# Sixteen score pairs and twenty-four matmul slots: two ways to lay out the gaps of a filled group

## The chip, the cores and the metric

The kernel runs on one core of one Trainium2 chip. The metric is the device time of one execution in microseconds. Before the change it is 1833.53 us, the median of three runs (1833.28 to 1835.45).

## The reference, cut to what matters

One transformer block on a sequence of S = 2048 rows of D = 512 in float32: 32 heads of 16, full softmax attention, then a gated feed-forward layer of width F = 1792. Both halves are modulated by vectors computed from a condition `c`.

```python
h = _layernorm(x, axis=-1) * (1 + ca) + sa
x = x + ga * _A_ref(h, A_wqkv, A_wo)     # scores = q k^T * scale; p = softmax(scores); (p v) @ wo
h = _layernorm(x, axis=-1) * (1 + cb) + sb
x = x + gb * _B_ref(h, B_w_gate, B_w_up, B_w_down)   # (silu(h w_gate) * (h w_up)) @ w_down
```

## The kernel before

**Attention.** The sequence is cut into NC = 4 chunks of CW = 512 query columns, the heads into NG = 8 groups of four. A unit is one group of four heads for one chunk; there are 32 units, and a unit has 16 steps, one for each tile of 128 keys. A step has four heads. For each head there is a *score* (`score`, lines 566 to 575): a matmul of 50 rows into one PSUM bank (L573), from which ScalarE (ACT) makes the exponential into SBUF (L575). Because the softmax subtracts a maximum of each query, each score needs a *max* matmul some 21 steps ahead (`LEAD`), in `max_one` (lines 515 to 526): a matmul of 48 rows into a bank (L524), which VectorE (DVE) reduces over its 512 columns (L526). The probabilities times V are matmuls of 32 columns each (`pv_step`, L588), four heads side by side.

**Pairs.** `pair_of` (line 983) issues one score and one max together. The two use opposite halves of the array's rows (0 to 63 and 64 to 127), so that they run side by side. There are 16 x 4 pairs to a unit.

**Banks.** `Turn` hands out banks in rotation. In a filled stretch the scores alternate between two banks, 4 and 5, and the maxima rotate over three, 0, 1 and 2 (`four, bank = three, Turn(4, 5)`, line 1066). So score k may only start when the exponential of score k-2 has read its bank, and max k when the reduce of max k-3 has.

**Plain and filled stretches.** After attention of a chunk is done, its output projection and feed-forward layer are worked off inside the attention of the next chunk. `plain` (line 1047) issues pairs and probability-times-V steps alone. `filled` (line 1062) issues pairs, and behind pair r it takes `places[r]` *slots* of other work; after the last pair come the postponed element-wise steps (`hook`) and a burst of `len(places) // 2 + 2` half-steps of probability times V:

```python
        for r in range(len(places)):
            pair_of()
            take(work, places[r])
            if r % 4 == 3:
                end_steps()
        hook()
        pvs(len(places) // 2 + 2, False)
```

A slot is one step of the generator `accumulate` with `halves=True` (line 785 on): two matmuls of 64 rows (L790), one in each row half, again side by side. A job of `gate_up` or `out_pair` has 24 slots: twelve terms in each of two phases. In the first phase the upper row half accumulates into one output bank and the lower into the other; in the second they change over. Where `trade` is set, the change-over needs a wait: a no-op on ACT (L799) waits for the last matmuls of the first phase, and the first matmuls of the second phase wait for that no-op.

`filled_tile` (line 1078) lays out a job of `gate_up` or `out_pair`. Normally it takes one group of sixteen pairs with the tuple `FOUR`, and trades; near the end of a unit and near the end of the kernel it takes two groups of eight pairs with `TWO`. A `down` job has 12 slots in a group of eight pairs with `DOWN = (0, 3, 3, 0, 3, 3, 0, 0)`, and trades as well. In `FOUR` before, the first phase of twelve slots ends behind pair 6, then come pair 7 with no slot and pair 8, and then the second phase starts.

After a gate-up job ACT makes a tanh (L863) and DVE two products (L867, L869) from the two output banks. Once in a unit the maxima found ahead are gathered (in filled stretches by `max_turned`, line 546): a small reduce on DVE, a scale on ACT (L564), two small steps on DVE and eight small DMAs, each hung on a pair.

All engines run in program order, so the order in which these functions issue is the order of the work on TensorE.

Of the kernel before, what the change touches and what calls it, by code (L numbers as in the profile page):

```python
# [50 lines left out]
STARTS = (147, 275, 403)  # L51
TWO = (0, 3, 2, 2, 2, 2, 1, 0)
DOWN = (0, 3, 3, 0, 3, 3, 0, 0)
FOUR = (0, 3, 2, 2, 2, 1, 2, 0, 2, 2, 2, 2, 2, 1, 1, 0)
ALONE = {TWO: (0, 4, 0, 4, 0, 4, 0, 0), DOWN: (0, 6, 0, 0, 0, 6, 0, 0)}


# [47 lines left out]
def block_kernel(ctx, tc, x, wqkv, wo, w_gate, w_up, w_down, c, w_mod, out):  # L105
# [956 lines left out]
    def filled(places, work):  # L1062

        nonlocal four, bank, beside
        beside = True
        four, bank = three, Turn(4, 5)
        if done >= 4 * n - 4 * (LEAD - 1):
            places, bank = ALONE.get(places, places), Turn(4, 5, 0, 1, 2)
# [7 lines that stand above are left out]
        turns_behind()  # L1076

    def filled_tile(job, ch, arg):
        one = done // 4 % 16 != 15 and done + 16 <= 4 * n - 4 * (LEAD - 1)
        work = job(ch, arg, outs, True, one)  # L1080
        for places in (FOUR,) if one else (TWO, TWO):
            filled(places, work)
# [115 lines left out]
```

## Time and profile before

| | |
|---|---|
| median of the runs | 1833.53 us |
| profiled execution, its own time | 1833.51 us |
| its span, first to last instruction | 1831.6 us |
| TensorE (PE) busy | 1820.9 us, 99% |
| VectorE (DVE) busy | 1516.8 us, 83% |
| ScalarE (ACT) busy | 1246.8 us, 68% |
| GpSimd (POOL) busy | 460.8 us, 25% |
| granted TensorE clock | 1.000 |

The page gives the busy time of each engine, and the chain of waits that ended last, followed back from the last instruction. PE is a matmul, PEld the load of its weights; a weight load carries the wait of its matmul. A timeline gives start and duration of each instruction; neighbours of the same kind on one engine are merged (x4), and in brackets stands the idle time of the engine ahead of it and what ended that. Matmuls overlap, so a matmul's duration is longer than its distance from the next one, and a delay is seen in the starts. A matmul that comes right behind its own weight load has a longer duration than one whose weights were loaded ahead.

### The profile page before, as it was taken

To read this page: it belongs to the slowest core of one execution; us is meant where nothing else is said; L and a number is where in the kernel's file an instruction comes from. 1 tells how busy PE (TensorE), PEld (TensorE's weight loads), DVE (VectorE), ACT (ScalarE), POOL (GpSimd) and SP (SyncE) were. 2 spreads that over 40 slices of the span, in tenths; PEclk is the share of its full clock that TensorE was granted. 3 is DMA by queue.
4 is the path that set the end of the run, shared out by engine and by line. 5 is a ranking of instruction groups with operands and counts; after the bars stand their busy time and mean duration, and the time that the engine had idled before them with its cause. 6 is when DMAs were issued, how large, how long until landed. Compare 5 with 4: busy or idle time off the path is not lost.

```text
span 1831.6 us, 41022 instructions
## 1 busy us (share of the span) xinstructions
PE 1820.9 (99%) x16898; PEld 1196.8 (65%) x16898; DVE 1516.8 (83%) x2556; ACT 1246.8 (68%) x2357; POOL 460.8 (25%) x538
## 2 busy tenths in 40 slices
PE   9999999999999999999999999999999999999999
PEld 7876444444465777776565777776564677677887
DVE  6578999999999888888989888898989988922544
ACT  4223888888888666676888776676888867773211
POOL 3612544556223111111123111111213111030200
PEclk9999999999999999999999999999999999999999
DMA  9884876667745454453545554444643565233742
GB/s 313 280 226 146 205 200 166 179 170 209 191 85 120 103 125 140 126 133 73 156 95 131 115 125 118 123 115 90 161 79 57 125 146 122 105 118 121 279 168 104
DMA packets 80596, 267.63 MB, mean 146 GB/s; under 512 B 19744, under 2 KB 24320, under 8 KB 59728
## 3 DMA queue, kind: packets, MB, share of 16 engines
q1 hardware_dynamic: 61432, 179.71, 33.9%
q0 software_dynamic: 18288, 84.49, 19.2%
q8 instruction: 133, 2.18, 0.5%
q10 hardware_dynamic: 688, 0.80, 0.1%
q14 instruction: 55, 0.45, 0.1%
HBM read 201.85 MB, written 62.13 MB: 144 GB/s over the span
## 4 chain that ended last, share of the span: by engine, by line
PE 83%; DVE 14%; ACT 2%; DMA 0%; issue 0%; SPq 0%; DVEq 0%
PE bank L588 21%; PE bank L790 19%; PE bank L573 15%; DVE mx L526 14%; PE bank L524 11%; PE bank L809 8%; PE bank L214 7%; PE bank L852 1%; PE bank L773 0%; DMA wm_ab<-in_w_mod 0%; PE bank L166 0%; ACT sq L833 0%; DVE v_flat L883 0%; PE bank L538 0%; ACT sq L829 0%
## 5 line engine op out<-in xcount | busy, mean ns | idle before, releaser
L526 DVE TENSOR_REDUCE mx<-bank 128x1 f32<-128x512 f32 x2048 | 1269.3, 681 | 121.9 <-PE bank L524 83.5
L573 PE MATMUL bank<-qop,kop 50*128 50x512 f32 x2048 | 739.8, 428 | 1.4 <-ACT pu__17793 L575 0.2
L524 PE MATMUL bank<-kop,qop 48*128 48x512 f32 x2048 | 729.6, 425 | 0.3
L573 PEld LDWEIGHTS bank<-qop,kop 50*128 50x128 f32 x2048 | 345.7, 184 | 181.1 <-issue 37.4
L524 PEld LDWEIGHTS bank<-kop,qop 48*128 48x128 f32 x2048 | 345.3, 184 | 108.5 <-DVE mx L526 61.9
L790 PE MATMUL bank<-act,wgu 64*128 64x512 f32 x1872 | 306.0, 392 | 0.0
L790 PEld LDWEIGHTS bank<-act,wgu 64*128 64x128 f32 x1872 | 194.4, 187 | 24.1
L614 POOL TENSOR_TENSOR rb<-o,rb 128x512 f32<-128x512 f32 x31 | 39.9, 1286 | 539.1 <-DMA rb<-d_dr 400.0
L790 PE MATMUL bank<-wd,mid 64*128 64x512 f32 x912 | 131.6, 391 | 0.0
L871 POOL CAST mid<-m 128x512 fp32r<-128x512 f32 x40 | 24.4, 611 | 357.9 <-DVE m L869 357.9
L790 PEld LDWEIGHTS bank<-wd,mid 64*128 64x128 f32 x912 | 91.4, 186 | 11.7
L214 PE MATMUL bank<-hT,wqs 128*128 128x512 f32 x384 | 94.2, 397 | 0.4 <-DVE wqs L354 0.4
L867 DVE SCALAR_TENSOR_TENSOR q<-th,bank 128x512 f32<-128x512 f32 x56 | 38.1, 680 | 54.1 <-ACT th L863 54.1
L214 PEld LDWEIGHTS bank<-hT,wqs 128*128 128x128 f32 x384 | 70.6, 188 | 18.8 <-issue 3.1
L863 ACT ACTIVATE th<-bank 128x512 f32<-128x512 f32 x56 | 33.3, 594 | 57.9 <-PE bank L809 57.9
L883 DVE TENSOR_TENSOR x<-bank,x 128x512 f32<-128x512 f32 x84 | 53.9, 685 | 16.1 <-PE bank L790 16.1
L869 DVE TENSOR_TENSOR m<-bank,q 128x512 f32<-128x512 f32 x56 | 38.7, 692 | 21.7 <-PE bank L809 19.7
L872 POOL TENSOR_TENSOR mid<-m,mid 128x512 fp32r<-128x512 f32 x40 | 51.4, 1285 | 3.3
L809 PE MATMUL bank<-wd,mid 128*128 128x512 f32 x216 | 51.3, 393 | 0.0
L790 PE MATMUL bank<-wgu,act 64*128 64x512 f32 x288 | 48.2, 392 | 0.0
L214 PE MATMUL bank<-wqs,hT 128*128 128x512 f32 x192 | 48.0, 398 | 0.0
L809 PEld LDWEIGHTS bank<-wd,mid 128*128 128x128 f32 x216 | 40.4, 188 | 8.9
(6300 smaller groups left out, 5143.6 us busy)
## 6 DMA issues: line engine op xcount, KB each, us to landing
wgu<-gu_dr SPq DMA_DIRECT2D x48, 1024.0 KB
wd<-wd_dr SPq DMA_DIRECT2D x28, 1024.0 KB
kop<-kd SPq DMA_DIRECT2D x33, 768.0 KB
kop<-kd POOLq DMA_DIRECT2D x29, 768.0 KB, 8.7
gu_dr<-wgu POOLq DMA_DIRECT2D x14, 1024.0 KB, 12.7
kd<-prt SPq DMA_DIRECT2D x16, 512.0 KB
qd<-prt SPq DMA_DIRECT2D x16, 512.0 KB
kop<-gu_dr SPq DMA_DIRECT2D x8, 1024.0 KB
```

The lines of the kernel that those rows point to most:

```text
L214: nc.tensor.matmul(pt, lhs(a, k), rhs(b, k), start=(n == 0), stop=(n == 3 * nk - 1))
L524: nc.tensor.matmul(pm, qop[u][rows, s, qt * P:(qt + 1) * P], kop[u % 3][rows, s, kc * CW:(kc + 1) * CW], start=True, stop=True)
L526: nc.vector.tensor_reduce(mx[u][:, b, s, qt, kc:kc + 1], pm, op=ALU.max, axis=AX.X)
L573: nc.tensor.matmul(sp, kop[u % 3][rows, h // 2, kt * P:(kt + 1) * P], qop[u][rows, h // 2, :], start=True, stop=True)
L588: nc.tensor.matmul(pv[u][32 * h:32 * h + 32, cols], v_flat[:, e0:e0 + 32], p_[h][:, cols], start=(kt == 0 and half == 0), stop=(kt == 15), ...
L614: mul.tensor_mul(rb, o, rb)
L790: mm = nc.tensor.matmul(outs[e], lhs(e, a, k)[rows], rhs(b, k)[rows], start=(ph == 0 and j == 0), stop=(j == z and (ph == 1 or trade)), sk ...
L809: nc.tensor.matmul(outs[e], lhs(e, a, k), rhs(b, k), start=(j == 0), stop=(j == z))
L867: nc.vector.scalar_tensor_tensor(q, th, 1.0, outs[0], op0=ALU.add, op1=ALU.mult)
L869: nc.vector.tensor_mul(m32, outs[1], q)
L872: (nc.gpsimd if slow else nc.vector).tensor_sub(mid[:, 1, :], m32, mid[:, 0, :].bitcast(F32))
L883: nc.vector.tensor_add(ch.x2[:, t, :], outs[e], ch.x2[:, t, :])
```

## The change

The tuple `FOUR` says how many slots stand behind each of the sixteen pairs of a group. The sum (24) stays, and so does the number of slots ahead of pair 7 (12).

```diff
-FOUR = (0, 3, 2, 2, 2, 1, 2, 0, 2, 2, 2, 2, 2, 1, 1, 0)
+FOUR = (0, 3, 2, 1, 2, 1, 3, 0, 3, 1, 2, 1, 2, 1, 2, 0)
```

Taken two at a time, the neighbouring gaps before held 3 5 4 4 3 3 2 2 4 4 4 4 3 2 1 slots; now they hold 3 5 3 3 3 4 3 3 4 3 3 3 3 3 2. Behind the last pair of a group comes the burst of probability-times-V steps in both.

## The prediction

> **What bounds the kernel now.** I read the page first, then the views of lines L799 and L790 for the count of the groups, then the timeline of one group of sixteen pairs, and last a timeline of the neighbouring kinds of group for the price of the new spacing.
>
> ```profile
> span 1831.6 us, 41022 instructions
> PE 1820.9 (99%) x16898; PEld 1196.8 (65%) x16898; DVE 1516.8 (83%) x2556; ACT 1246.8 (68%) x2357; POOL 460.8 (25%) x538
> ...
> PE 83%; DVE 14%; ACT 2%; DMA 0%; issue 0%; SPq 0%; DVEq 0%
> ...
> L526 DVE TENSOR_REDUCE mx<-bank 128x1 f32<-128x512 f32 x2048 | 1269.3, 681 | 121.9 <-PE bank L524 83.5
> ```
>
> TensorE's order of instructions sets the end: 83% of the chain is PE. A "busy" PE at 99% hides small delays, because two row halves overlap; they have to be found in the starts. DVE is 14% of the chain, from the plain stretches, which this change leaves alone.
>
> How many groups does it touch? The trade of the banks leaves one ACT no-op (L799) in every group that trades: the FOUR groups and the down groups.
>
> ```profile
> L799 ACTq EVENT_SEMAPHORE x74: 17/17/17, 531.7 to 1662.7; - x74
> ```
> ```profile
> L790 PE MATMUL bank<-wd,mid x912: 384/392/471, 628.6 to 1664.1; 64*128 64x512 f32 x183
> ```
>
> A down job in halves is 12 slots of two matmuls: 912/24 = 38 jobs. So 74 - 38 = 36 FOUR groups use the edited tuple.
>
> Now one of them, from its first pair at 641.63 us. I number pairs from 0 and call gap k the slots behind pair k. First its start, then pairs 6 to 9 around the trade, then pairs 13 to 15 and the probability-times-V burst (L588) up to the next group.
>
> ```profile
> 641.63 0.50 PE L573 MATMUL bank<-qop,kop 50*128 50x512 f32 x1
> ...
> 641.97 0.39 PE L573 MATMUL bank<-qop,kop 50*128 50x512 f32 x1
> ...
> 642.20 1.89 DVE L526 TENSOR_REDUCE mx<-bank 128x1 f32<-128x512 f32 x3 [0.32 <-PE bank L524]
> ```
> ```profile
> 645.47 0.60 ACT L575 ACTIVATE pt__7527<-bank 128x512 f32<-128x512 f32 x1
> 645.48 0.42 PE L573 MATMUL bank<-qop,kop 50*128 50x512 f32 x1
> ...
> 645.74 0.64 PE L790 MATMUL bank<-act,wgu 64*128 64x512 f32 x4
> 645.96 0.60 ACT L575 ACTIVATE pt__7536<-bank 128x512 f32<-128x512 f32 x1
> ...
> 646.20 0.40 PE L524 MATMUL bank<-kop,qop 48*128 48x512 f32 x1
> ...
> 646.61 0.18 PEld L573 LDWEIGHTS bank<-qop,kop 50*128 50x128 f32 x1 [0.31 <-ACT pt__7536 L575]
> ...
> 646.62 0.50 PE L524 MATMUL bank<-kop,qop 48*128 48x512 f32 x1
> ...
> 646.95 0.64 PE L790 MATMUL bank<-act,wgu 64*128 64x512 f32 x4
> ...
> 647.31 0.18 PEld L573 LDWEIGHTS bank<-qop,kop 50*128 50x128 f32 x1 [0.17 <-ACT pu__7546 L575]
> ...
> 647.42 0.39 PE L573 MATMUL bank<-qop,kop 50*128 50x512 f32 x1
> ```
> ```profile
> 650.23 0.39 PE L573 MATMUL bank<-qop,kop 50*128 50x512 f32 x1
> ...
> 650.66 0.60 ACT L575 ACTIVATE pt__7598<-bank 128x512 f32<-128x512 f32 x1
> ...
> 651.16 0.39 PE L524 MATMUL bank<-kop,qop 48*128 48x512 f32 x1
> 651.31 0.18 PEld L573 LDWEIGHTS bank<-qop,kop 50*128 50x128 f32 x1 [0.19 <-ACT pt__7598 L575]
> 651.31 0.49 PE L573 MATMUL bank<-qop,kop 50*128 50x512 f32 x1
> ...
> 651.73 0.40 PE L588 MATMUL bank<-pt__7427,v_flat 128*32 128x256 f32 x1
> ...
> 653.21 0.69 DVE L869 TENSOR_TENSOR m<-bank,q 128x512 f32<-128x512 f32 x1
> ...
> 655.32 0.18 PEld L573 LDWEIGHTS bank<-qop,kop 50*128 50x128 f32 x1 [0.41 <-issue]
> ...
> 655.89 0.69 DVE L526 TENSOR_REDUCE mx<-bank 128x1 f32<-128x512 f32 x1 [1.99 <-PE bank L573]
> ```
>
> The pace: from pair 1 (641.97) to pair 7 (646.20) lie 6 pairs and 3+2+2+2+1+2 = 12 slots, so 4.23/18 = 0.235 us for each, pair or slot; call it a beat.
>
> The limit: scores alternate between two banks, so score k needs the exp of score k-2 done. For pair 8: score 6 starts at 645.48, its exp at 645.96 (0.48 later), runs 0.60, the weight load starts at 646.61 (0.05 later), and the matmul that comes straight behind its load takes 0.50 instead of 0.39 to 0.40, so everything behind is another 0.10 late. That path is 0.48 + 0.60 + 0.05 + 0.10 = 1.23 us. Gaps 6 and 7 hold 2 + 0 slots, so pair 8 has its turn 4 beats = 0.94 after pair 6: 0.29 us late. The rows show both parts: 646.62 instead of 646.20 + 0.235 is 0.19, and the next slot comes 0.33 after the pair (646.95) instead of 0.235, 0.10 more. Pair 9 (647.42) comes on its beat, two beats behind the slot at 646.95, although gaps 7 and 8 hold only two slots: the delay of pair 8 already paid for it.
>
> For pair 15: score 13 at 650.23, exp at 650.66, 0.43 later: here ACT was free, whereas exp 6 stood behind exp 5 (645.47), 0.49 between starts. The path is 1.18. Gaps 13 and 14 hold 1 + 1, again 0.94: late by 0.24. The rows: the max of the pair at 651.16, its score at 651.31, 0.15, plus the 0.10 of its 0.49 us.
>
> **The change part by part.** No instruction is added or removed: 24 slots and 16 pairs stay, and so does the place of the trade, behind 12 slots, with pairs 7 and 8 before the second half. No DMA and no other queue is moved past another; work that is hung on a pair keeps its pair. Sums of neighbouring gaps become 3 at pairs 2, 4, 5, 6, 8, 9, 11, 12, 13, 14 and 15 and more elsewhere; before, they were 2 at pairs 8, 9 and 15, and 3 at pairs 2, 6, 7 and 14. Only the last gaps (2 + 0) stay under 3, and behind them lies the burst of 3.59 us (651.73 to 655.32).
>
> 1. Removed: 0.29 at pair 8 and 0.25 at pair 15, 0.54 us per group. If all of it went, 36 x 0.54 = 19.4 us.
>
> 2. Given back: a sum of 3 is 5 beats = 1.175 us, and the path is 1.18 with ACT free and 1.23 behind a gap of one. So a window of three is no cover with room: it costs 0.005, or 0.055 where score k-2 stands directly behind a single slot (pairs 6, 8, 12, 14). Being late itself undoes that: pair 6, late by 0.055, leaves ACT time to be free again, so pair 8 then pays the small price; so for 12 and 14. Two at 0.055 and nine at 0.005 make 0.155; before paid some 0.02 for its four, none of them with score k-2 behind a single slot. Net 0.13.
>
> Is a window of three around the trade as cheap as I say? The down groups have it already: three slots, a pair, a pair, three slots, with the trade.
>
> ```profile
> 670.37 0.41 PE L573 MATMUL bank<-qop,kop 50*128 50x512 f32 x1
> ...
> 670.81 0.60 ACT L575 ACTIVATE pt__7863<-bank 128x512 f32<-128x512 f32 x1
> ...
> 671.32 0.65 PE L573 MATMUL bank<-qop,kop 50*128 50x512 f32 x2
> 671.47 0.18 PEld L573 LDWEIGHTS bank<-qop,kop 50*128 50x128 f32 x1 [0.19 <-ACT pt__7863 L575]
> ...
> 671.55 0.41 PE L524 MATMUL bank<-kop,qop 48*128 48x512 f32 x1
> ...
> 671.80 0.86 PE L790 MATMUL bank<-wd,mid 64*128 64x512 f32 x6
> ```
>
> Score 2 of that group (670.37), exp at 670.81, load at 671.47, so the score is as late as if it had begun at 671.57. Its max runs at 671.55, a beat behind the pair before (671.32), and the slots at 671.80 instead of some 671.74: 0.06 paid, for the window and the trade together. The trade's wait has lost pair 8's delay as cover, and this row holds all of that. Between 0.005 and 0.06 at pair 8 I take the middle, 0.03, so another 0.02. Bound below zero: excluded, a beat is not shortened by the order.
>
> 3. A disturbance: in some groups ACT runs a small scale of the maxima between exp 5 and exp 6.
>
> ```profile
> 659.20 0.40 PE L573 MATMUL bank<-qop,kop 50*128 50x512 f32 x1
> ...
> 659.65 0.21 ACT L564 ACTIVATE parts<-m 128x16 fp32r<-128x16 f32 x1
> ...
> 659.76 0.59 ACT L575 ACTIVATE pt__7718<-bank 128x512 f32<-128x512 f32 x1
> ```
>
> Score 6 to exp 6 is 0.56 here, the path 1.31: a window of three pays 0.13 at pair 8 where it would pay 0.03. The scale occurs sixteen times in all:
>
> ```profile
> L564 ACT ACTIVATE parts<-m x16: 206/208/218, 605.0 to 1611.9; 128x16 fp32r<-128x16 f32 x16
> ```
>
> So 16 x 0.10 = 1.6 us against the change at most once each (between 0 and 3, if DVE's share of the same work also makes a max wait).
>
> 4. DVE: two of its reduces start 0.60 apart back to back ((1.89 - 0.68)/2), and where gaps alternate 1 and 2 a pair comes every 2.5 beats = 0.59, so DVE falls behind by only 0.01 per pair. Three banks hold the maxima: pair 15 needs reduce 12, which starts at the earliest 0.57 + 12 x 0.60 = 7.8 us into the group (642.20 - 641.63 is the 0.57) and is done, with 0.68 and 0.15 of handover, at 8.6; pair 15 is due at 0.34 + 38 x 0.235 = 9.3. Cost 0. At the group's end DVE idles 1.99 us before the next group's first max, so a group that ends 0.4 us earlier still doesn't wait for q and m (653.21 + 0.69 against 655.32). If that cover were gone, the gain would be lost one for one.
>
> Sum: 36 x (0.54 - 0.13 - 0.02) = 14.0, less 1.6, makes 12.4 us. The burst follows the group on the same engine, so it passes to the end in full. The profiled execution took 1833.51 us around its span of 1831.6, and the median is 1833.53, so the sum stands against either: 1833.5 - 12.4, or 1821 us.
>
> **The rivals.** *Full cure.* The windows of three cost nothing, as pair 9 above starts on its beat with its load only 0.11 ahead (647.31, 647.42). Then 19 us go: 1814. Against it: the down row's 0.06.
>
> *The wait is spread, not removed.* Seven windows of three, one behind the other (into pairs 2, 4, 6, 8, 11, 13, 15), each pay the down row's 0.06 or a little more, 0.07: 7 x 0.07 = 0.49 of 0.54 comes back, and 36 x 0.05 leaves 1831.7, no change. For it: the path of 1.18 is above 1.175 at every one of them. Against it: pair 6 of the quoted group has a window of three (2 + 1), and the slots behind its score come 0.26 later (645.48, 645.74), 0.02 over a beat. The Trainium skill, Perfetto Trace Analysis, section Optimization Strategy, says that a gap which repeats on the engine that should be full can mean too little PSUM for the next tile; by that, spacing without a third score bank would only move the wait, and this rival's time follows. The trace agrees that the wait is for one of two banks, but its beat shows that a window of three nearly covers it.
>
> *Slower.* The single slots keep ACT behind, group-wide: exp after exp finds ACT still busy, and the path at those seven windows is the 1.31 of the disturbed group instead of 1.18. That costs 7 x 0.135 = 0.95 per group against 0.54: 36 x 0.41 = 15 us, 1848. It decides from a path of 1.175 + 0.54/7 = 1.25 on. Against it: exps start 0.49 apart and pairs come 0.59 apart on average, so ACT catches up.
>
> That the edit doesn't do what it says: the sums above, counted, show that it does; no chance of its own.
>
> **How the numbers follow.** The forecast 0.76, the full cure 0.13, spread 0.08, slower 0.03. About 0.2%, 3.7 us, is what a measurement of this kernel can tell from no change; the first two cases lie beyond it, and I leave 0.02 of the forecast's own lower tail to no change. The range reaches from the full cure, 1814, to 1828: a give-back of 0.06 at five windows, 0.30 instead of 0.15, with 3 us for the disturbances, leaves 0.24 x 36 - 3 = 5.6 us.
>
> **What would show it.** Groups of 13.69 us (641.63 to 655.32) should take about 13.3; the PE wait at pair 8 should be under 0.1 us of delay, and pair 15's score should start with its max. Small waits for exp should appear at pairs 6 and 12. DVE's idle of 1.99 before a group should shrink to some 1.6. Down groups and plain stretches should be the same. Wrong would be: groups at 13.6 or more, or PE waiting for DVE inside them.

## The result, and the profile after

The changed kernel takes 1820.6 us, the median of six runs (1820.0 to 1822.87), beside 1834.34 us before in the same sessions (six runs, 1833.2 to 1836.8). The ratio is 0.9927, with a 95% interval of 0.9914 to 0.994: that is 13.4 us faster. The forecast was 12.4 us faster, or 1821 us, in a range from 1814 to 1828.

The head of the page of the changed kernel, with the chain of waits:

```profile
span 1821.1 us, 41022 instructions
...
PE 1809.9 (99%) x16898; PEld 1181.1 (65%) x16898; DVE 1507.0 (83%) x2556; ACT 1234.9 (68%) x2357; POOL 459.9 (25%) x538
...
PE 96%; DVE 2%; ACT 2%; DMA 0%; issue 0%; SPq 0%; DVEq 0%; ACTq 0%
```

Two things here mislead. First, the span fell by 10.5 us only. The profiled execution of the changed kernel took 1822.87 us, the longest of its six, and was 2.6 us late before the first score. The view of line L573 gives the first and the last score of the whole kernel, before and then after:

```profile
L573 PE MATMUL bank<-qop,kop x2048: 383/398/504, 167.0 to 1666.8; 50*128 50x512 f32 x187
```
```profile
L573 PE MATMUL bank<-qop,kop x2048: 383/398/505, 169.6 to 1656.3; 50*128 50x512 f32 x187
```

From first to last score 1499.8 us before, 1486.7 after: 13.1 less, and that is what the change can touch.

Second, DVE's share of the chain fell from 14% to 2%. That is no gain: outside of the groups of sixteen the two traces differ by less than 0.1 us from the first to the last score. That PE and DVE are about equally late in the plain stretches, so that the chain goes along one or the other, is a reading of this and not shown by itself. In the chain of before most DVE pieces stand there, for instance this one, long before the first group of sixteen at 526.92:

```profile
207.28 23.41 DVE mx L526 x39
```

The sum of the 36 groups of sixteen pairs, each taken from its first pair to the first pair of what follows, tells where the time went. First the sum of before, then of after, from the view by windows (the sum of the 36 stretches stands first, then busy times):

```profile
sum 494.96, PE 494.16 PEld 364.45 DVE 424.95 ACT 355.24 POOL 76.45; mean PE 13.73 PEld 10.12 DVE 11.80 ACT 9.87 POOL 2.12
```
```profile
sum 481.90, PE 481.85 PEld 348.91 DVE 415.21 ACT 343.42 POOL 74.61; mean PE 13.38 PEld 9.69 DVE 11.53 ACT 9.54 POOL 2.07
```

494.96 - 481.90 = 13.06 us, 0.363 per group: all of the 13.1. Nothing was lost on the way to the end and nothing came from elsewhere; the 34 full down groups take 6.82 us each in both traces.

Now the same group in the timeline of the changed kernel, where it starts at 642.68 us: pairs 2 to 4, then pairs 6 to 8, then pair 15, the burst and the next group:

```profile
643.96 0.41 PE L573 MATMUL bank<-qop,kop 50*128 50x512 f32 x1
...
644.41 0.60 ACT L575 ACTIVATE pt__7500<-bank 128x512 f32<-128x512 f32 x1
...
645.06 0.18 PEld L573 LDWEIGHTS bank<-qop,kop 50*128 50x128 f32 x1 [0.20 <-ACT pt__7500 L575]
...
645.12 0.44 PE L524 MATMUL bank<-kop,qop 48*128 48x512 f32 x1
...
645.40 0.40 PE L790 MATMUL bank<-act,wgu 64*128 64x512 f32 x2
```
```profile
646.36 0.41 PE L573 MATMUL bank<-qop,kop 50*128 50x512 f32 x1
...
646.81 0.60 ACT L575 ACTIVATE pt__7534<-bank 128x512 f32<-128x512 f32 x1
...
647.31 0.65 PE L573 MATMUL bank<-qop,kop 50*128 50x512 f32 x2
647.46 0.18 PEld L573 LDWEIGHTS bank<-qop,kop 50*128 50x128 f32 x1 [0.20 <-ACT pt__7534 L575]
...
647.80 0.63 PE L790 MATMUL bank<-act,wgu 64*128 64x512 f32 x4
```
```profile
652.05 0.40 PE L524 MATMUL bank<-kop,qop 48*128 48x512 f32 x1
652.08 0.39 PE L573 MATMUL bank<-qop,kop 50*128 50x512 f32 x1
652.40 0.40 PE L588 MATMUL bank<-pt__7427,v_flat 128*32 128x256 f32 x1
...
655.99 0.18 PEld L573 LDWEIGHTS bank<-qop,kop 50*128 50x128 f32 x1 [0.41 <-issue]
...
656.56 0.69 DVE L526 TENSOR_REDUCE mx<-bank 128x1 f32<-128x512 f32 x1 [2.00 <-PE bank L524]
```

The group takes 13.31 us (642.68 to 655.99) instead of 13.69. Pair 15 starts whole (652.05, 652.08), and the burst comes 0.35 behind it, where it came 0.57 behind. Pair 8 still waits for exp 6: the bracket at 647.46 is as large as many before, but the load is only 0.06 before the matmul's turn instead of 0.18 after it, and just 0.05 is lost. Pair 4, which did not wait before, now does (645.06), and the slot behind it comes 0.28 after the pair instead of a beat of 0.235.

### The profile page after: what moved, and what is told of

Its sections match the earlier page's. It is cut to its first block, busy times and chain, and to the rows that moved or that the text cites. A ratio compares the mean times of both kernels' runs of the same rounds, so it can differ in the third digit from the quotient of the medians.

```text
span 1821.1 us, 41022 instructions
## 1 busy us (share of the span) xinstructions
PE 1809.9 (99%) x16898; PEld 1181.1 (65%) x16898; DVE 1507.0 (83%) x2556; ACT 1234.9 (68%) x2357; POOL 459.9 (25%) x538
## 4 chain that ended last, share of the span: by engine, by line
PE 96%; DVE 2%; ACT 2%; DMA 0%; issue 0%; SPq 0%; DVEq 0%; ACTq 0%
PE bank L588 26%; PE bank L790 20%; PE bank L573 18%; PE bank L524 15%; PE bank L809 8%; PE bank L214 7%; DVE mx L526 2%; PE bank L852 1%; PE bank L773 0%; DMA wm_ab<-in_w_mod 0%; PE bank L166 0%; ACT sq L833 0%; PE bank L538 0%; DVE v_flat L883 0%; PE bank L537 0%
## 5 line engine op out<-in xcount | busy, mean ns | idle before, releaser
L573 PE MATMUL bank<-qop,kop 50*128 50x512 f32 x2048 | 732.2, 427 | 0.6 <-ACT pu__17793 L575 0.2
L573 PEld LDWEIGHTS bank<-qop,kop 50*128 50x128 f32 x2048 | 345.5, 184 | 192.0 <-issue 37.4
```

The source lines that it names most:

```text
L573: nc.tensor.matmul(sp, kop[u % 3][rows, h // 2, kt * P:(kt + 1) * P], qop[u][rows, h // 2, :], start=True, stop=True)
```

## The experiments

Each run is timed against the kernel before on the same chip. The table gives that ratio and, as the finer instrument, the sum of the 36 groups of the run's own trace; the change's is 481.90, that of before 494.96.

| run | ratio to before, 95% interval | sum of the 36 groups, us |
|---|---|---|
| the change | 0.9927 (0.9914 to 0.994) | 481.90 |
| trade alone | 0.9961 (0.9947 to 0.9975) | 488.23 |
| end alone | 0.9956 (0.9943 to 0.9969) | 488.72 |
| halves in turn | 0.9946 (0.9932 to 0.9959) | 484.20 |
| third score bank, new gaps | 0.9864 (0.9848 to 0.9881) | 475.39 |
| third score bank, old gaps | 0.9895 (0.9881 to 0.9908) | 479.97 |
| four slots into pair 12 | 0.9937 (0.9923 to 0.995) | 481.48 |
| longer path on ACT | 0.9984 (0.9975 to 0.9993) | 490.57 |
| two banks for maxima | 1.0165 (1.0151 to 1.0179) | 512.17 |
| halves exchanged | 0.9939 (0.9923 to 0.9956) | 482.73 |

**The two places apart.** Around the trade alone:

```diff
-FOUR = (0, 3, 2, 1, 2, 1, 3, 0, 3, 1, 2, 1, 2, 1, 2, 0)
+FOUR = (0, 3, 2, 1, 2, 1, 3, 0, 3, 1, 2, 2, 2, 1, 1, 0)
```

> Gaps (0,3,2,1,2,1,3,0,3,1,2,2,2,1,1,0): the windows around the trade hold three slots, the two gaps ahead of pair 15 hold 1 + 1 as before. Theory A (two score banks, each short window is paid for on its own): pair 8's 0.33 us of delay falls to 0.07, pair 4 pays a new 0.06 to 0.07, pair 15 stays 0.24 late; 0.19 to 0.2 us per group, so 7 us faster than before (1826.5), and 6 to 7 us slower than the change. Rival B (only the trade's wait matters): all of the change's 13 us, 1820.5. Rival C (only the group's end matters, where DVE and the next burst follow): no change, 1833.5.

At the group's end alone:

```diff
-FOUR = (0, 3, 2, 1, 2, 1, 3, 0, 3, 1, 2, 1, 2, 1, 2, 0)
+FOUR = (0, 3, 2, 2, 2, 1, 2, 0, 2, 2, 2, 1, 2, 1, 2, 0)
```

> Gaps (0,3,2,2,2,1,2,0,2,2,2,1,2,1,2,0): around the trade 2 + 0 and 0 + 2 as before, the end as in the change. Theory A: pair 15's 0.22 us goes, pair 12 pays a new 0.05, pair 8 stays at 0.33; 0.17 us per group, 6 us faster than before (1827.5). Rival B: no change, 1833.5. Rival C: all of the gain, 1820.5. The gains of this run and of the trade alone should add up to the change's 13 us by theory A.

The sums of the groups, first with the trade alone, then with the end alone:

```profile
sum 488.23, PE 488.19 PEld 357.89 DVE 419.13 ACT 347.05 POOL 77.01; mean PE 13.56 PEld 9.94 DVE 11.64 ACT 9.64 POOL 2.14
```
```profile
sum 488.72, PE 487.94 PEld 357.52 DVE 420.40 ACT 351.79 POOL 75.17; mean PE 13.55 PEld 9.93 DVE 11.68 ACT 9.77 POOL 2.09
```

6.73 us and 6.24 us less than before, together 12.97 of the change's 13.06. Each short window was paid for on its own, and neither rival holds. Averaged over the groups, the first keeps 0.22 at the end and has 0.07 at pairs 4 and 8; the second keeps 0.32 at pair 8 and pays 0.05 behind pair 12: the terms, one by one, as expected.

**A third bank for the scores.** With the new gaps, and then with the old ones:

```diff
-        four, bank = three, Turn(4, 5)
+        four, bank = Turn(0, 1), Turn(4, 5, 2)
...
-        nc.vector.tensor_reduce(mx[u][:, b, s, qt, kc:kc + 1], pm, op=ALU.max, axis=AX.X)
+        nc.vector.tensor_reduce(mx[u][:, b, s, qt, kc:kc + 1], pm[:, 0:CW // 2] if filling else pm, ...)
```

> The change's gaps, in filled groups three banks for scores and two for maxima; so that two banks are enough for the maxima, their reduce in filled groups reads 256 of 512 columns, and the exponential's scale is an eighth. Left out: half of each maximum's columns there. Theory A: no weight load of a score waits for an exp in the groups of sixteen any more; a group is 40 beats of 0.235 with some 0.1 at either end, about 9.6 us, and the burst of 3.59, 13.2 us instead of 13.39; with 0.06 less in 34 down groups 8 to 9 us faster than the change, 1811 to 1813. This is the ceiling for any spacing. Rival D (DVE's pace sets the groups, not the scores' banks): with a third less work on DVE much more than that, groups under 13 us, 1805 or less; or, if the banks of scores do not matter, no gain over the change.

> The gaps of before, with three banks for scores and two for maxima in filled groups, the reduce there over 256 of 512 columns and an eighth of the exponential's scale. Left out: half of each maximum's columns there. Theory A (the gaps matter only through the two banks of scores): the waits at pairs 8 and 15 vanish without any new spacing, groups of 13.2 us and 1810 to 1812 in all, the same as the change's gaps with three banks. Rival (the trade's wait or the order of slots at the group's end costs by itself): groups longer than 13.3, 4 us or more over that.

First the sum with the new gaps, then with the old:

```profile
sum 475.39, PE 475.16 PEld 358.21 DVE 295.65 ACT 344.17 POOL 80.06; mean PE 13.20 PEld 9.95 DVE 8.21 ACT 9.56 POOL 2.22
```
```profile
sum 479.97, PE 479.74 PEld 376.52 DVE 296.50 ACT 351.77 POOL 79.22; mean PE 13.33 PEld 10.46 DVE 8.24 ACT 9.77 POOL 2.20
```

With the new gaps a group takes 13.20 us as worked out, and no delay is left behind pairs 4, 8 and 12. Relative to before, the run is 1.36% faster: 25 us, or 11.6 beyond the change, which is 3 more than expected. The groups of sixteen give 6.5 of it, the 34 down groups 0.1 each (6.72 instead of 6.82), so 3.3, and the twelve TWO groups 0.8. DVE's work in the groups fell by 120 us (415.21 to 295.65), and only 6.5 of that is gained, so DVE's pace did not set them.

With the old gaps the expected 13.2 was missed by 0.13 per group. The delay at pair 8 is gone with no new spacing, so the trade has no wait of its own there. At pair 15 one remains (0.12, averaged), but for another reason. Its max, in the old gaps with two banks for maxima:

```profile
649.30 0.79 DVE L527 TENSOR_REDUCE mx<-bank 128x1 f32<-128x256 f32 x2 [0.27 <-PE bank L525]
...
649.77 0.18 PEld L525 LDWEIGHTS bank<-kop,qop 48*128 48x128 f32 x1 [0.25 <-DVE mx L527]
```

The load of the max (L525 there) waits for the reduce of two pairs before: the experiment's own two banks met the short window 1 + 1. So this run shows it for pair 8 and leaves pair 15 to the run with the end alone and to the one with the new gaps. The Trainium skill, Perfetto Trace Analysis, section Optimization Strategy, takes a repeated gap on the engine that should be full as a possible sign of too little SBUF or PSUM for the next tile. These two runs agree for the scores (13.20 and 13.33 us per group instead of 13.39 and 13.75). But a bank for the scores has to come from somewhere:

```diff
-        four, bank = three, Turn(4, 5)
+        four, bank = Turn(0, 1), Turn(4, 5, 2)
```

> The change, with three banks for scores and two for maxima in filled groups, whole reduces. Theory A: the scores' waits go (0.19 us per group), but a max now needs the reduce of the max two pairs earlier: 0.43 + 0.68 + 0.15 = 1.26 us at least against a window of 1.175, and DVE's 0.60 per reduce against 0.59 per pair adds up; 0.4 to 0.8 us more per group, also in the down groups, 10 to 25 us slower than the change, 1830 to 1846. Rival (a third bank of scores is worth more than the third of maxima): 5 us or more faster than the change.

This is 30 us slower than before and 44 slower than the change, where 10 to 25 had been expected. The groups of sixteen cost 30.3 of it (512.17 instead of 481.90, 0.84 each where at most 0.8 was expected) and the 34 down groups 10.6 (7.13 us each instead of 6.82). The max of pair 4 there, its reduce, and the load of the max of pair 6:

```profile
647.28 0.48 PE L524 MATMUL bank<-kop,qop 48*128 48x512 f32 x1
...
647.99 1.91 DVE L526 TENSOR_REDUCE mx<-bank 128x1 f32<-128x512 f32 x3
...
648.67 0.18 PEld L524 LDWEIGHTS bank<-kop,qop 48*128 48x128 f32 x1 [0.40 <-DVE mx L526]
```

Averaged over the groups the delays are about 0.15 to 0.3 into each of pairs 2, 6, 10 and 14. I had priced the path (1.26 us) with a free DVE, whose reduce starts 0.43 behind its max. Here reduce 4 starts 0.71 behind it, because DVE still has earlier work in hand; averaged over the groups it is 0.57 to 0.87 at pairs 0, 4, 8 and 12, on which these waits hang, and 0.43 again at pairs 3, 7, 11 and 15. Whole maxima need their third bank more than the scores do.

**A longer path.**

```diff
         nc.scalar.activation(p_, sp, AF.Exp, scale=SCALE)
+        if filling:
+            nc.scalar.mul(extra, ident[:, 0:16], -1.0)
```

> The change, and behind each exp in filled groups one more small ScalarE instruction (128 x 16, of the size of the scale of the maxima, 0.21 us, 0.11 to the next start), so that an exp behind a gap of one or none starts some 0.11 later. Theory A (the path from score k-2 over its exp to score k is as long as a window of three): waits of 0.1 or so into pairs 6, 8, 10 and 12, 0.2 to 0.4 us more per group, 8 to 14 us slower than the change, 1829 to 1835. Rival (ScalarE, busy 68%, has room to take it): within 2 us of the change.

Pairs 8 to 12 of one group, from exp 8 on; L577 is the exp, L579 the added instruction, L575 the score:

```profile
648.10 0.59 ACT L577 ACTIVATE pt__7656<-bank 128x512 f32<-128x512 f32 x1
...
648.68 0.60 ACT L577 ACTIVATE pt__7668<-bank 128x512 f32<-128x512 f32 x1
...
648.74 0.50 PE L575 MATMUL bank<-qop,kop 50*128 50x512 f32 x1
...
649.18 0.21 ACT L579 ACTIVATE extra<-ident 128x16 f32<-128x16 f32 x1
...
649.28 0.59 ACT L577 ACTIVATE pt__7678<-bank 128x512 f32<-128x512 f32 x1
...
649.93 0.18 PEld L575 LDWEIGHTS bank<-qop,kop 50*128 50x128 f32 x1 [0.19 <-ACT pt__7678 L577]
```

Score 10 (648.74) waits for exp 8 (648.10 and 0.59), exp 10 starts 0.54 behind it instead of 0.45, and pair 12 waits for exp 10. The sum is 490.57, 8.7 us more than the change's, and by the ratios the run is 10.5 slower, as theory A had it. ACT is busy 72% of the span, and still the 0.1 per exp is paid. But exps now follow each other back to back, about 0.60 apart, beside the pairs' 0.59, and between the exps of a group ACT idles 0.24 us, averaged, instead of 1.02 in the change. So the run does not tell a longer path from an ACT that has become too slow for the pairs.

**Which windows of three are paid for.** The prediction had the waits at pairs 6 and 12, from ACT's backlog behind a single slot. The trace of the change has them at 4, 8 and 12. In `pair_of` the scores of pairs 0 and 1 of each four run in rows 0 to 63, those of 2 and 3 in rows 64 to 127, and the lower half's matmul is issued first. So into pair 4, 8 or 12 the window goes from a score in the second half to one in the first. The run with the halves in turn:

```diff
-        h = (ORDER if done < most else (0, 1, 2, 3))[done % 4]
+        h = (ORDER if done < most and not turn_ else (0, 1, 2, 3))[done % 4]
+        r = done + 4 * (LEAD - 1)
+        if turn_:
+            r += (0, 1, -1, 0)[done % 4]
...
-            work.insert(1 - h % 2, lambda: max_one(done + 4 * (LEAD - 1)))
+            work.insert(1 - h % 2, lambda: max_one(r))
```

> The change's gaps, but in filled groups the scores take the row halves in turn (0, 64, 0, 64 instead of 0, 0, 64, 64), and the maxima the other ones, so that score k and score k-2 run in the same half. Theory H (the waits at pairs 4, 8 and 12 come because score k-2 ran in the half that is some 0.03 us behind and second of its pair, while score k is first of its pair in the half that is ahead): the waits of 0.06 at pairs 4, 8, 12 and at pair 4 of the down groups fall to 0.03 or less, groups from 13.39 to 13.25 to 13.35 us, 2 to 5 us faster than the change, 1816 to 1818.5. Rival (backlog of ACT behind a single slot, as the prediction had it, or the place of the pair in the group): the same waits at the same places, or 0.02 to 0.03 at every window; within 1 us of the change.

The waits did not stay at three places, but the sum did not fall: 484.20, 2.3 us more than the change. In the same half a window of three has 1.175 against 1.18 or so, and seven windows now pay 0.02 to 0.06 each (pairs 2, 4, 6, 8, 10, 12 and 14, 0.26 per group) where three paid 0.05 to 0.07 (0.19). Theory H's saving was wrong; from the first half to the second there is room, and without the change of halves that room is lost. A little at every second window is also near to what the rival expected, so this run does not decide between them.

A window of four into pair 12:

```diff
-FOUR = (0, 3, 2, 1, 2, 1, 3, 0, 3, 1, 2, 1, 2, 1, 2, 0)
+FOUR = (0, 3, 2, 1, 2, 1, 3, 0, 3, 1, 2, 2, 1, 2, 1, 0)
```

> The change with its second half laid out (3,1,2,2,1,2,1,0): the window into pair 12 holds four slots, those into pairs 11, 13, 14 and 15 three. Theory A with the row halves (a window of three costs 0.05 to 0.07 only into pairs 4, 8 and 12, whose score is in the half that is ahead while score k-2 was in the half behind): pair 12's 0.05 us goes, nothing comes for it, groups from 13.39 to 13.33 or 13.34 us, 1.5 to 2 us faster than the change. Rival (every window of three costs about as much, or ACT is late behind a single slot, as the prediction had it): a wait moves to pair 14 or 15, groups as in the change.

Nothing was gained: 481.48, and a ratio within the interval of the change's. Pair 12's wait is gone and pair 13 has it. Score 11, its exp, and the load of score 13:

```profile
646.89 0.40 PE L573 MATMUL bank<-qop,kop 50*128 50x512 f32 x1
...
647.35 0.60 ACT L575 ACTIVATE pu__7580<-bank 128x512 f32<-128x512 f32 x1
...
648.00 0.18 PEld L573 LDWEIGHTS bank<-qop,kop 50*128 50x128 f32 x1 [0.21 <-ACT pu__7580 L575]
```

I had overlooked that scores 11 and 13 stand in the same relation, second half to first. In the change pair 13 escapes because pair 12 has just been late. The last run puts this to the test by exchanging the halves in filled groups:

```diff
-        h = (ORDER if done < most else (0, 1, 2, 3))[done % 4]
+        h = ((1, 3, 0, 2) if turn_ else ORDER if done < most else (0, 1, 2, 3))[done % 4]
+        r = done + 4 * (LEAD - 1)
+        if turn_:
+            r += (2, 2, -2, -2)[done % 4]
```

> The change's gaps, but in filled groups the row halves are exchanged: scores in 64, 64, 0, 0 instead of 0, 0, 64, 64, the maxima opposite. Theory H, as the earlier runs left it (a window of three costs some 0.05 us where score k-2 ran in the half behind and score k runs in the half ahead, unless the pair before it has just been late): the waits leave pairs 4, 8 and 12 and come into pairs 2 or 3, 6, 10 or 11, and 14 or 15; in the down groups from pair 4 to pair 2 or 7. In all 0.15 to 0.25 us per group as before, so within 3 us of the change. Rival (the waits belong to these places in the group, to the trade or to the gaps ahead of them): waits stay at pairs 4, 8 and 12.

The delays are now behind pairs 2, 6, 10, 11 and 14 (0.06, 0.05, 0.04, 0.03 and 0.05), none behind 4, 8 or 12; the sum is 482.73. In a down group the wait is at pair 2, where it had been at pair 4 (the row at 671.47 in the prediction):

```profile
669.72 0.60 ACT L575 ACTIVATE pt__7847<-bank 128x512 f32<-128x512 f32 x1 [3.13 <-PE bank L573]
...
670.38 0.18 PEld L573 LDWEIGHTS bank<-qop,kop 50*128 50x128 f32 x1 [0.23 <-ACT pt__7847 L575]
```

So the place in the group and the trade do not decide which windows wait, and a single slot ahead is not needed for it; the order of the two row halves decides. In all of these runs the lower half's matmul is also issued first, so what the row half does and what the order of issue does is not told apart. Of the runs that leave nothing out, none was faster than the change beyond the intervals.

## Why the prediction was right

*The count.* 36 groups, and the gain lies in them alone.

*What was removed.* 0.54 us per group was forecast, read from one group. Averaged over the 36 groups, the delay at pair 8 and behind it was 0.32 (0.29 in the one that was quoted; the disturbed ones have more), at the end 0.22 (0.25 forecast): 0.54.

*What was given back.* Forecast 0.13 net for the windows and 0.02 for the trade's surroundings; measured 0.07 + 0.07 + 0.05 = 0.19 less next to nothing before. The size was nearly right, with the down group's row as the best witness: its 0.06 is what each of the three pays. The places were right in part (pair 12 waits, but 4 and 8 do instead of 6), and the cause that I gave, ACT's backlog behind a single slot, was wrong. At the exps for which pairs 4, 8 and 12 wait no backlog shows: exp 6 starts 0.45 behind its score (646.36, 646.81), as exp 2 does, which stands behind three slots (643.96, 644.41). A backlog does show at exps 4 and 12 (0.50 and 0.49 behind their scores, averaged, and as much with the third bank), but pairs 6 and 14, which need these, pay nothing.

*The disturbance.* 1.6 us against the change was the mis-sized term; it is nearly nil. I had charged the scale of the maxima to the new gaps, but the old ones paid it as well: with it a group takes 13.78 us instead of 13.69 before (the groups from 655.32 and 641.63 in that trace), and 13.42 instead of 13.31 after. Averaged, it cancels but for 0.02 or so per such group; and of the sixteen scales only eight fall between exps 5 and 6 of a group of sixteen. This and the larger give-back (0.18 per group by the third bank, 0.15 forecast) hid each other: 36 x (0.54 - 0.18) = 13.0 against 12.4. That the sum came so close is in part luck.

*DVE.* No max waited, as forecast, but for pair 1 of four groups, in both traces alike. But DVE's idle time before the next group is 2.00 us, not 1.6. The last max of the group now comes earlier as well, so DVE ends earlier by as much as the group does.

*The rivals.* The full cure (19 us) failed on the 0.06 of the down row; the third bank shows what was left of it, 0.18 per group. The spread (no gain) failed since a window that pays delays the scores behind it, and so gives the next window its room, as pair 13 shows, which waits only when pair 12 does not. The slower case did not occur, but the run with the longer path comes near its mechanism: with 0.1 more per exp, exp after exp finds ACT busy, and most of the gain is gone.

## What to carry to other kernels

Where work alternates between two buffers, compare the whole path from one use to its release (matmul, exp, wake-up, weight load) with the sum of the *two* gaps that it spans, not with the average rate: here a pair of gaps one slot short cost more than one slot's time, and all slots could be kept. Then move slots from windows with room to those without, and expect the waits to come back, smaller, where a window just reaches the path. An engine that is a third idle (ACT was busy 68% before) can still set the pace through its latency.

## What the runs showed of the hardware

- A matmul whose weight load had to wait past the matmul's turn costs its delay and 0.10 us besides: it takes 0.49 to 0.50 us instead of 0.39 (pairs 8 and 15 before, 646.62 and 651.31), and what follows on the engine is late by that too. A load that ends its wait 0.05 to 0.06 us before the matmul's turn costs 0.05 (pair 4 after, 645.06 and 645.12); one 0.11 before costs nothing (pair 9 before, 647.31 and 647.42).
- Two matmuls in opposite row halves do not always start together: in the change the second half starts up to 0.04 us behind (pair 15 above by 0.03, 652.05 and 652.08), and its exp starts some 0.45 after the matmul instead of 0.43 (averaged, pairs 3, 7 and 11 against 5, 9 and 13; with the halves exchanged, pairs 3 and 7 have 0.43). Exchanging the halves changed which of several equal windows wait (4, 8 and 12; then 2, 6, 10, 11 and 14).
